# Dynamic convolution and squared-ReLU FFN on one core: second softmax part ahead of the first conv, its input loaded second, row moves on one queue a sub-block, blocks 0 to 4 reordered

## The chip, the cores and the metric

The kernel runs on one core of one Trainium2 chip. The metric is the time of one execution on the device, in microseconds (us). Each execution also reports the mean clock that the throttle granted to TensorE.

## The reference, cut to what matters

```python
# attention part: softmax of the given weights over K = 7 taps, then a causal dynamic convolution
w = softmax(weight_gen, axis=-1)                    # B=8, S=4096, H=8, K=7
out[b, s, h] = sum_k w[b, s, h, k] * x_pad[b, s + k, h]     # groups of 24 of the 192 channels
# FFN part, on 32768 tokens
h = maximum(x @ w_in, 0)                            # 192 -> 2048
return (h * h) @ w_out                              # 2048 -> 192
```

## The kernel before

The sequence is cut into 64 sub-blocks of 512 tokens. Blocks 0 and 1 hold one sub-block each, all later blocks two. For each sub-block, softmax weights (`exp` on ScalarE, called ACT; sum, reciprocal and products on VectorE, called DVE) are moved into rows by small DMAs (`wr`), DVE multiplies the rows by a band mask (`bd`), and TensorE (PE) convolves by matrix products with these bands (`C`, result `y`). A unit `u` is the first product for 256 columns of the FFN's hidden layer in blocks 0 and 1 and 128 in later ones (PE writes `h`, ACT applies ReLU to give `t`, DVE squares it to `g`). `M` is one half of a quarter's second product, collected in two PSUM banks `o`. The kernel spells out the order of these steps in strings.

The first sub-blocks get their softmax in small parts (`s0`, `s1`, `s2`: 8 rows for each of 128 partitions, with a halo of 6). The start of the program:

```python
spin(25)                        # idle products of 128x512, to keep TensorE busy
half_swap(); band_mask(); nc.gpsimd.memset(v_big, 0.0)
s0.load(nc.sync)                # 392 KB
load_w_in(w_st[0], 0, nc.sync)  # 768 KB in three DMAs
x_load_f32(0)                   # 480 KB
load_w_in(w_st[1], 1, nc.sync)  # 768 KB
s0.exp(0, s0.rh); s0.total(0, s0.rh); s0.recip(0, s0.rh); s0.scale(0, s0.rh, nc.vector)
nc.scalar.copy(out=w_i[:, 0, 0], in_=w_st[0])
wr_load_sbuf(0, [s0], (0, 2, 1, 4, 3), (nc.sync, nc.gpsimd))   # rows of sub-block 0: 5 DMAs of 16 KB
wr_load_sbuf(1, [s0], range(NT), (nc.gpsimd,))                 # rows of sub-block 1
x_cast(0, nc.scalar.copy)
cross_w_in_by_pe(0)
spin(14)
x_load_f32(1)
nc.scalar.copy(out=w_i[:, 1, 0], in_=w_st[1])
cross_w_in(1)
s1.load(nc.sync)                # the second softmax part's input, 392 KB, behind 16 other DMAs of SyncE
for i in (0, 2, 1, 3, 4):
    st_band(0, (i,))
st_conv(0)
# ... cut: loads of w_out, s2 and x ...
steady = "MuMuuu" * 3 + "MuuuMCu"
plans = {     # B bands, X cast of x, E exp, S rest of softmax, L load, C conv of the next block
    0: "B1 X1 u u u E1 S1 u C u u u u",
    1: "L3 u u B2 M E2 B3 u M E2 u u S2 u M u C u S2 M",
    2: "L4 u u u E3 M u u u M B4 u u u u M B5 S3 u u u u M u E3 C u",
    3: "L5 L6 M S3 u u u M u u u u M u M B6 E4 u u u M M B7 u u S4 u E4 M u C M u",
}
```

The M step that closes a quarter is followed by the copy that frees its banks:

```python
def o_sum(j, qt, ccs, o):
    # ... cut ...
    nc.scalar.copy(out=o_sb, in_=o[0][:, c])
    if len(o) == 2:
        nc.vector.tensor_tensor(out=o_sb, in0=o[1][:, c], in1=o_sb, op=AluOp.add)
```

The softmax here doesn't subtract the row's maximum and nothing guards it: scores larger than these inputs give would overflow.

## Time and profile before

| | before |
|---|---|
| time, median of 4 runs (three first, one more with the changed kernel) | 747.84 us (747.12 to 748.63) |
| span of the profiled run | 746.6 us, granted clock 1.000 |
| first useful matmul (conv 0) | 13.04 us |
| first unit | 15.55 us |
| start of the convs of blocks 2, 5, 6 | 33.13, 98.79, 121.34 us |

A row of a timeline is: start in us, length in us, engine, line of the kernel, operation, output and inputs, how many; in brackets, how long the engine was idle before it and what ended that. The prediction below shows the rows that carry it. ACT's timeline, for the arrival of w_in:

```profile
3.93 0.93 ACT L217 ACTIVATE ex<-wg 128x784 f32<-128x784 f32 x1 [1.83 <-DMA wg<-in_weight_gen_dram]
7.03 1.47 ACT L558 CAST w_i<-w_st 128x1536 f16<-128x1536 f32 x1 [2.17 <-DMA w_st<-in_moe_w_in_dram]
11.29 1.49 ACT L565 CAST w_i<-w_st 128x1536 f16<-128x1536 f32 x1
```

The first half of w_in is in at 7.0 us. The tile `wr` in the window from 8 to 12.2 us: the row moves by issuing engine, and how long they took from issue to landing (shortest, median, longest):

```profile
L330 POOL DMA_DIRECT2D wr<-v_first x7: 523/537/687, 8.6 to 11.8; - x7
L330 SPq DMA_DIRECT2D wr<-v_first x3: 597/598/636, 8.3 to 9.6; - x3
...
DMA to landing us min/median/max: 2.4/2.9/3.5
```

### The profile page before, as it was taken

Reading aid. Unit: us, or ns where it says so; the run is one execution under the profiler, and the core shown is the slowest. Engines: PE = TensorE matmul, PEld = TensorE weight load, DVE = VectorE, ACT = ScalarE, POOL = GpSimd, SP = SyncE. Lnnn points to the kernel's source line nnn. Section 1 sums busy time; section 2 is a strip of 40 time slices with the busy share of each in tenths; the row PEclk is TensorE's granted clock in tenths of the full one; section 3 lists DMA queues with packets and bytes.
Section 4 is the critical chain, followed back from the end, with each engine's and each line's share of the span. In section 5 each row is a group of like instructions: output and inputs, shape, how many; then the busy total and the mean of one; then the engine's idle time right before and its main releaser. Section 6 shows DMA issues by size and latency. Waiting matters only on the chain.

```text
span 746.6 us, 33289 instructions
## 1 busy us (share of the span) xinstructions
PE 739.0 (99%) x15106; PEld 556.5 (75%) x15106; DVE 621.8 (83%) x1001; ACT 624.7 (84%) x755; POOL 88.8 (12%) x130
## 2 busy tenths in 40 slices
PE   8999999999999999999999999999999999999998
PEld 4767877877777777777777777787777777777787
DVE  5999998998889888888889888898888987677853
ACT  5998788888888888888888888888888888888874
POOL 7321220101101100011000110001100011001000
PEclk9999999999999999999999999999999999999999
DMA  8654454436554234644245542365441354441312
GB/s 223 112 106 109 80 101 85 100 70 139 94 118 79 75 57 80 140 79 73 45 74 139 102 65 53 51 139 108 59 80 48 57 108 80 60 73 51 51 46 65
DMA packets 122169, 64.81 MB, mean 87 GB/s; under 512 B 83849, under 2 KB 118636, under 8 KB 121516
## 3 DMA queue, kind: packets, MB, share of 16 engines
q1 hardware_dynamic: 77708, 45.66, 22.4%
q0 software_dynamic: 44176, 16.93, 20.5%
q8 instruction: 118, 1.93, 1.1%
q14 instruction: 23, 0.19, 0.1%
q10 hardware_dynamic: 144, 0.10, 0.0%
HBM read 48.61 MB, written 28.70 MB: 104 GB/s over the span
## 4 chain that ended last, share of the span: by engine, by line
PE 94%; DVE 2%; issue 1%; DMA 1%; ACT 1%; POOL 0%; DVEq 0%; ACTq 0%
PE o L475 45%; PE h L441 43%; PE yp L416 6%; DVE g L453 1%; DVE bd L348 1%; DMA wr<-v_first 0%; DMA wg<-in_weight_gen_dram 0%; POOL wr L330 0%; ACT t L450 0%; DVE v_first L239 0%; ACT ex L217 0%; DVE ssum L224 0%; DVE rcp L231 0%; DVE o_sb L491 0%; ACT y L427 0%
## 5 line engine op out<-in xcount | busy, mean ns | idle before, releaser
L450 ACT ACTIVATE t<-h 128x1024 f16<-128x1024 f32 x512 | 496.7, 1026 | 65.6 <-PE h L441 65.3
L453 DVE TENSOR_TENSOR g<-t 128x1024 f16<-128x1024 f16 x512 | 334.3, 687 | 100.5 <-ACT t L450 97.8
L475 PEld LDWEIGHTS <-g 64*128 64x128 f16 (+1 forms) x8032 | 352.3, 94 | 55.0 <-issue 4.8
L475 PE MATMUL o<-w_o,g 64*128 64x192 f16 (+1 forms) x8032 | 385.3, 243 | 0.9 <-DVE o_sb L491 0.6
L441 PE MATMUL h<-y,w_i 64*128 64x512 f16 (+1 forms) x3168 | 379.7, 370 | 2.2 <-ACT t L450 0.9
L441 PEld LDWEIGHTS <-w_i 64*128 64x128 f16 x3168 | 162.6, 94 | 117.2 <-issue 5.2
L348 DVE TENSOR_TENSOR bd<-wr,mask 128x4160 f16<-128x4160 f16 (+3 forms) x89 | 149.3, 1701 | 4.0 <-DMA wr<-v_first 4.0
L300 POOL DMA_DIRECT2D xt<-in_x_dram x62 | 51.2, 830 | 446.7 <-PE yp L416 423.7
L489 ACT COPY o_sb<-o 128x384 f32<-128x384 f32 x129 | 62.2, 482 | 33.8 <-PE o L475 33.8
L491 DVE TENSOR_TENSOR o_sb<-o,o_sb 128x384 f32<-128x384 f32 x123 | 68.2, 555 | 8.4 <-ACT o_sb L489 5.6
L427 ACT CAST y<-yp 128x1024 f16<-128x1024 f32 (+1 forms) x64 | 48.1, 803 | 14.5 <-PE yp L416 14.5
L416 PE MATMUL yp<-bd,xt 128*32 128x104 f16 (+8 forms) x3864 | 51.7, 208 | 0.3 <-DVE bd L348 0.2
L416 PEld LDWEIGHTS <-xt 128*32 128x32 f16 (+3 forms) x3864 | 46.2, 92 | 6.7 <-issue 6.2
L239 DVE TENSOR_TENSOR v_big<-ex,rcp 128x112 f16<-128x112 f32 (+1 forms) x136 | 27.3, 263 | 1.8 <-DMA vd<-v_big 0.6
L217 ACT ACTIVATE ex<-wg 128x448 f32<-128x448 f32 (+2 forms) x44 | 27.2, 618 | 1.8 <-DMA wg<-in_weight_gen_dram 1.8
L224 DVE TENSOR_REDUCE ssum<-ex 128x64 f32<-128x448 f32 (+2 forms) x44 | 26.1, 594 | 2.5 <-ACT ex L217 2.3
L231 DVE RECIPROCAL rcp<-ssum 128x64 f32<-128x64 f32 (+2 forms) x44 | 23.7, 539 | 1.5
L290 POOL DMA_DIRECT2D xt<-in_x_dram x7 | 3.8, 549 | 135.8 <-PE yp L416 135.8
L330 POOL DMA_DIRECT2D wr<-v_first x31 | 16.8, 561 | 16.3 <-DVE v_first L239 16.1
L539 PE MATMUL wp<-warm 128*128 128x512 f16 x39 | 11.4, 459 | 1.3 <-DVE warm L531 1.3
L539 PEld LDWEIGHTS <-warm 128*128 128x128 f16 x39 | 4.3, 114 | 7.6 <-issue 3.5
L239 DVE TENSOR_TENSOR v_first<-ex,rcp 128x112 f16<-128x112 f32 (+1 forms) x48 | 9.1, 255 | 0.3
(24 smaller groups left out, 28.2 us busy)
## 6 DMA issues: line engine op xcount, KB each, us to landing
out_dram<-o_sb SPq DMA_DIRECT2D x63, 384.0 KB, 3.0
xt<-in_x_dram POOLq DMA_DIRECT2D x42, 240.0 KB, 5.9
wg<-in_weight_gen_dram SPq DMA_DIRECT2D x4, 1064.0 KB, 8.3
xt<-in_x_dram POOLq DMA_DIRECT2D x20, 192.0 KB, 5.6
wr<-vd SPq DMA_DIRECT2D x38, 80.0 KB, 3.6
vd<-v_big SPq DMA_DIRECT2D x5, 512.0 KB, 5.5
wg<-in_weight_gen_dram SPq DMA_DIRECT2D x5, 392.0 KB
wg<-in_weight_gen_dram SPq DMA_DIRECT2D x3, 616.0 KB, 4.1
```

Of the source, the lines that this page charges most:

```text
L217: nc.scalar.activation(out=self.ex[:, lo:hi].rearrange("p r g k e -> p (r g) k e"), in_=self.wg[:, lo:hi].rearrange("p r (g e) k -> p (r g ...
L239: eng.tensor_tensor(out=bass.AP(tensor=v.tensor, offset=v.offset + lo * H * SL + lo % SL * 2 + g * SL * 2, ap=[list(v.ap[0]), [H * SL + 2, ...
L300: eng.dma_start(out=dst[:, first:last], in_=ap)
L348: nc.vector.tensor_tensor(out=bd_t[j][:, H * lo : H * (lo + len(tiles) * n)].rearrange("p (g m c) -> p g m c", g=shape[1], c=2 * SL), in0= ...
L416: nc.tensor.matmul(out=yps[k // per][p0 : p0 + m, col + a : col + b], lhsT=x_t[s][:, i, 32 * q : 32 * q + m], rhs=bd[:, h // 2, h % 2, a - ...
L427: nc.scalar.copy(out=y[:, k0:k1, 0:th], in_=yp[:, 0 : (k1 - k0) * th].rearrange("p (k c) -> p k c", c=th),)
L441: nc.tensor.matmul(out=h[:, half, jj * th : (jj + 1) * th], lhsT=w_in_chunk(u * per + jj, slot, half), rhs=y_t[j][r0 : r0 + RT, k, 0:th], ...
L450: nc.scalar.activation(out=t1, in_=h, func=ActF.Relu)
L453: nc.vector.tensor_tensor(out=g, in0=t1, in1=t1, op=AluOp.mult)
L475: nc.tensor.matmul(out=oo[:, cc * Dm : (cc + 1) * Dm], lhsT=g[r0 : r0 + n, cc * P : (cc + 1) * P], rhs=w_o[r0 : r0 + n, fc, :], start=(fc ...
L489: nc.scalar.copy(out=o_sb, in_=o[0][:, c])
L491: nc.vector.tensor_tensor(out=o_sb, in0=o[1][:, c], in1=o_sb, op=AluOp.add)
```

## The change

Its intent: DVE waits 3.3 us at the start for rows. The second part's softmax is to fill this hole, which takes an exp and 3.3 us of DVE work out of block 0. For this its input is loaded second. The rows of sub-blocks 0 to 3 each go through one queue, GpSimd's and SyncE's in turn. Blocks 0 to 4 get other orders, with an M already in block 0. (The diff's first hunk only takes the tile of the exps from a pool with two buffers in place of one.)

```diff
--- before.py
+++ after.py
@@ -205,7 +205,7 @@
         def exp(self, lo, hi):
 
             if lo == 0:
-                self.ex = self.tile(p_one, p_one, "ex", HK, "ex8").rearrange(
+                self.ex = self.tile(p_one, p_sm, "ex", HK, "ex8").rearrange(
                     "p (r g k e) -> p r g k e", g=HP, k=KK, e=2
                 )
                 self.ssum, self.rcp = (
@@ -544,6 +544,7 @@
         band_mask()
         nc.gpsimd.memset(v_big, 0.0)
         s0.load(nc.sync)
+        s1.load(nc.sync)
         w_st = [
             p_wg.tile([P, (R + HALO) * HK], f32, name="w_st", tag="wg")[:, 0 : NQ + NQ // 2]
             for q in (0, 1)
@@ -551,21 +552,23 @@
         load_w_in(w_st[0], 0, nc.sync)
         x_load_f32(0)
         load_w_in(w_st[1], 1, nc.sync)
-        s0.exp(0, s0.rh)
-        s0.total(0, s0.rh)
-        s0.recip(0, s0.rh)
-        s0.scale(0, s0.rh, nc.vector)
+        for s in (s0, s1):
+            s.exp(0, s.rh)
+            s.total(0, s.rh)
+            s.recip(0, s.rh)
+            s.scale(0, s.rh, nc.vector)
         nc.scalar.copy(out=w_i[:, 0, 0], in_=w_st[0])
-        wr_load_sbuf(0, [s0], (0, 2, 1, 4, 3), (nc.sync, nc.gpsimd))
-        wr_load_sbuf(1, [s0], range(NT), (nc.gpsimd,))
+        wr_load_sbuf(0, [s0], range(NT), (nc.gpsimd,))
+        wr_load_sbuf(1, [s0], range(NT), (nc.sync,))
         x_cast(0, nc.scalar.copy)
         cross_w_in_by_pe(0)
         spin(14)
         x_load_f32(1)
         nc.scalar.copy(out=w_i[:, 1, 0], in_=w_st[1])
         cross_w_in(1)
-        s1.load(nc.sync)
-        for i in (0, 2, 1, 3, 4):
+        wr_load_sbuf(2, [s0, s1], range(NT), (nc.gpsimd,))
+        wr_load_sbuf(3, [s0, s1], range(NT), (nc.sync,))
+        for i in range(NT):
             st_band(0, (i,))
         st_conv(0)
 
@@ -578,12 +581,13 @@
 
 
 
+        orders = {4: "MuuuMuuuMMuuMuuMuuMuuuMCu"}
         steady = "MuMuuu" * 3 + "MuuuMCu"
         plans = {
-            0: "B1 X1 u u u E1 S1 u C u u u u",
-            1: "L3 u u B2 M E2 B3 u M E2 u u S2 u M u C u S2 M",
-            2: "L4 u u u E3 M u u u M B4 u u u u M B5 S3 u u u u M u E3 C u",
-            3: "L5 L6 M S3 u u u M u u u u M u M B6 E4 u u u M M B7 u u S4 u E4 M u C M u",
+            0: "B1 X1 u u u u C B2 u u u M u",
+            1: "L3 u u u B3 M u u u E2 S2 M u E2 S2 C u M",
+            2: "L4 u u u M E3 u B4 u u M u u u B5 u M u u u u M u C S3 M E3 u",
+            3: "L5 L6 u u u M S3 u u u M M u u M B6 M u B7 u u u M E4 u u M u S4 C u",
         }
 
 
@@ -596,9 +600,9 @@
         PIECE = 8
 
         TIMES = {
-            (1, 0): ((3, 15), (4, 0)),
+            (1, 0): ((3, 15), (4, 3)),
             (1, 1): ((4, 15), (5, 0)),
-            (1, 2): ((4, 1), (5, 1), (5, 15)),
+            (1, 2): ((4, 6), (5, 1), (5, 15)),
             (2, 0): ((6, 1), (6, 15), (7, 0)),
             (2, 1): ((7, 9), (7, 15), (8, 15)),
             (3, 0): ((9, 9), (9, 15), (10, 9), (10, 15), (11, 0)),
@@ -608,7 +612,7 @@
 
             if u == 0:
                 return j - 1, 12
-            return j, {1: 0, 7: 3, 9: 4, 15: 8}[u]
+            return j, {1: 0, 3: 1, 6: 4, 7: 3, 9: 4, 15: 8}[u]
 
         for n, s in enumerate(parts):
             piece = s.rh if n < 2 else PIECE
@@ -629,12 +633,12 @@
         for j in range(len(plans), NBLK - 1):
             a = BLOCKS[j + 1][0]
             small = [p for p in parts if p.fb <= j + 1][-1].r == FIRST
-            us = {6: (7, 9)}.get(j, (5, 9) if small else (1, 5))
+            us = {4: (10, 12), 6: (7, 9)}.get(j, (5, 9) if small else (1, 5))
             for n, u in enumerate(us):
                 at(j, u, "B", a + n)
         for j in range(len(plans), NBLK):
             plan, u = [], 0
-            for step in steady:
+            for step in orders.get(j, steady):
                 if step == "u":
                     plan += [f"{kind}{n}" for kind, n in fill.get((j, u), ())]
                     u += 1
```

## The prediction

> **What bounds the kernel now.** I read the page first: busy shares, then the chain that ended last.
>
> ```profile
> PE 739.0 (99%) x15106; PEld 556.5 (75%) x15106; DVE 621.8 (83%) x1001; ACT 624.7 (84%) x755; POOL 88.8 (12%) x130
> ...
> PE 94%; DVE 2%; issue 1%; DMA 1%; ACT 1%; POOL 0%; DVEq 0%; ACTq 0%
> ```
>
> TensorE (PE) is busy 99% of 746.6 us and is 94% of the chain. The granted clock is 9 tenths or more in all 40 slices. So the program is TensorE work plus a start, and the question is how much of the stretch that the change touches is not TensorE work at its own pace. The timeline of PE gives the pace. In the steady stretch (here blocks 5 and 6) each row starts when the one before it has been issued, so I take differences of starts, not the durations, whose ends are modelled:
>
> ```profile
> 102.95 1.48 PE L475 MATMUL o<-w_o,g 64*128 64x192 f16 x32
> 104.27 2.11 PE L441 MATMUL h<-y,w_i 64*128 64x512 f16 x18
> 106.21 1.48 PE L475 MATMUL o<-w_o,g 64*128 64x192 f16 x32
> ...
> 121.34 1.57 PE L416 MATMUL yp<-bd,xt 128*32 128x104 f16 x120
> 122.84 0.82 PE L441 MATMUL h<-y,w_i 64*128 64x512 f16 x6
> ```
>
> An M step (half a quarter of the second product) takes 104.27 - 102.95 = 1.32 us, three u steps (units of the first product) 1.94 us, so 0.65 each, and a conv C of two sub-blocks 1.50 us. A steady block, 16 u + 8 M + C = 10.35 + 10.56 + 1.50 = 22.4 us; convs of later blocks start 22.55 us apart (144.41, 166.96, 189.52). Nothing is left to win after block 6, and the diff doesn't touch it. The loss must sit in the start and in blocks 0 to 4. The PE timeline of the start and of block 0:
>
> ```profile
> 9.92 3.19 PE L539 MATMUL wp<-warm 128*128 128x512 f16 x14
> 13.04 0.51 PE L416 MATMUL yp<-bd,xt 128*32 128x104 f16 x26
> 13.72 0.94 PE L416 MATMUL yp<-bd,xt 128*32 128x104 f16 x46 [0.17 <-DVE bd L348]
> 15.55 2.80 PE L441 MATMUL h<-y,w_i 64*128 64x256 f16 x48 [0.89 <-ACT y L427]
> 18.41 0.91 PE L416 MATMUL yp<-bd,xt 128*32 128x104 f16 x72
> 19.32 0.83 PE L441 MATMUL h<-y,w_i 64*128 64x256 f16 x12
> 21.05 4.28 PE L441 MATMUL h<-y,w_i 64*128 64x256 f16 x60 [0.90 <-ACT t L450]
> 25.26 1.50 PE L475 MATMUL o<-w_o,g 128*128 128x192 f16 x16
> ```
>
> The reader is to see three things. Useful work starts at 13.04 (conv 0) and the units at 15.55. At 20.15 PE waits 0.90 us for ScalarE (ACT), all three PSUM buffers of h being full. Then 5 units (60 matmuls) take 25.26 - 21.05 = 4.21 us where 5 x 0.69 = 3.45 would do (0.69 from 28.88 to 30.95, 36 matmuls = 3 units): 0.76 us more, ACT's pace of 0.95 us a unit. After 25.26 PE has one more wait in the touched part, of 0.62 us in block 4 (below). Check by a sum, from the first unit (15.55) to the conv of block 6 (121.34), 105.8 us: 16 u x 0.69 + 63 u x 0.65 + conv 1 at 0.91 + 4 C x 1.50 + 8 M of the first two blocks at 1.43 + 24 M x 1.32 = 11.0 + 41.0 + 0.9 + 6.0 + 11.4 + 31.7 = 102.0. So the excess is 3.8 us: 0.90 + 0.76 + 0.62 = 2.3 are the waits named, 1.5 is small change at transitions, about 0.1 each. **2.3 us, 0.3% of the time, is all that the reordering can openly win.**
>
> **What the Trainium skill says.** "Perfetto Trace Analysis", Identifying the Most-Contended Engine: matmul busy share is no measure of the distance to the peak; gaps are to be sought stage by stage. The trace agrees: between 21.05 and 25.26 PE is shown busy while it runs at 3.45/4.21 of its pace. "DMA: Bandwidth & Descriptors", Issuing engines are not separate DMA queues: issuing from several engines saves only the sequencer's issue time, as all run on the same 16 DMA engines. In the trace a row move takes 0.55 us to issue on GpSimd and 0.60 on SyncE. The same page, Anatomy of one DMA: some 2.0 us fixed per DMA. Here a 16 KB row move lands 1.7 to 3.9 us after its issue, median 2.5, and about 3.0 at 8.3 us, when loads still fill the DMA engines (share 0.94 to 1.10 from 3 to 10 us).
>
> **The change part by part.**
>
> 1. Second softmax part moved ahead of conv 0. Removed from block 0: on ACT one exp of 128x784 (0.95 us), on VectorE (DVE) the sum 0.97, the reciprocal 0.85 and eight products 1.45 = 3.3 us. Put where? These rows of the DVE timeline tell:
>
> ```profile
> 6.79 1.46 DVE L239 TENSOR_TENSOR v_first<-ex,rcp 128x112 f16<-128x112 f32 x8
> 11.57 2.60 DVE L348 TENSOR_TENSOR bd<-wr,mask 128x832 f16<-128x832 f16 x5 [3.32 <-DMA wr<-v_first]
> 14.89 2.36 DVE L348 TENSOR_TENSOR bd<-wr,mask 128x3328 f16<-128x3328 f16 x2 [0.73 <-DMA wr<-v_first]
> ```
>
> DVE is idle 8.25 to 11.57, 3.32 us, for the rows to land; 3.3 us of softmax fits to within 0.1. On ACT there is a wait from 4.87 to 7.03 for w_in, and the exp (0.95) fits in it if its input has come. So nearly free at both ends.
>
> 2. The input of it loaded second: 392 KB more ahead of w_in and x on SyncE's queue. From 3.91 (first input) to 7.03 (first half of w_in, 768 KB) the queue moves 250 KB/us, so what follows comes 1.2 to 1.5 us later (estimate): the w_in cast on ACT starts at about 8.4 instead of 7.03, x's cast ends at 10.8 instead of 9.4, PE's swap products and the 14 spins end at about 13.9 instead of 13.1, the second w_in cast ends at about 13.8 instead of 12.78. All of these still end before the last band of conv 0 (next point), so they are hidden, with little to spare.
>
> 3. Row moves on one queue a sub-block. Before, conv 0's five moves were split, 3 on SyncE and 2 on GpSimd, issued within 1.9 us. Now all five are GpSimd's: 8.55 + 0.69 + 4 x 0.55 = 11.4 for the last issue's end, landing about 2.5 to 2.9 after its start (10.85): 13.5. Its band, 0.55 us, ends at about 14.2 (five bands from 11.6 in row would end at 14.17, as before). So conv 0 ends at about 14.8 against 14.66. Sub-block 1 gains: its moves go from SyncE at 8.3 rather than GpSimd at 9.8, so the 0.73 us wait at 14.89 goes. First unit at 15.55 + 0.2 (range 0 to +0.8): **+0.2**.
>
> 4. Block 0 in its new order, worked out from the first unit at 15.75 with ACT at 0.95 a unit and y at 0.82, PE at 0.69, three h buffers: ACT's four outputs end at 17.55, 18.5, 19.45, 20.4, y at 21.2. PE: four u to 18.55, conv 1 to 19.46, u to 20.16, u waits for 20.4, u waits for 21.2 and ends 21.9. Here the plan puts an M (1.43) where before there was none until ten units were done; ACT catches up meanwhile. Then u, and three u of block 1, to 26.1, M. 11 u + conv 1 + M = 7.6 + 0.9 + 1.4 = 9.9 us of work in 10.35: a loss of 0.45 in place of 1.66. **-1.2.** DVE takes the bands of sub-blocks 2 and 3 (2.3 us each) earlier, with the 3.3 us less; t1 has 5 buffers, so DVE may lag by several units before ACT stalls.
>
> 5. Blocks 3 and 4 in another order. The wait in block 4:
>
> ```profile
> 77.57 0.24 PE L475 MATMUL o<-w_o,g 64*128 64x192 f16 x1
> 78.43 1.48 PE L475 MATMUL o<-w_o,g 64*128 64x192 f16 x31 [0.62 <-DVE o_sb L491]
> ```
>
> An M that opens a quarter needs both o banks. They come free 1.53 us after the closing M ended (76.85 to DVE's add ending 78.38), and only one u (0.72) lay between. The new order puts u, C, u there (2.8 us): **-0.6**. But it has two u only (1.30 us) after a closing M in three places, one in block 3 and two in block 4: 1.53 - 1.30 = 0.23 each, more where DVE lags: **+0.6** for all three. M counts by the end of block 4 are 24 in both, u and C are the same.
>
> Sum: +0.2 - 1.2 - 0.6 + 0.6 = -1.0 us. From 748.4: **747.3 us**, with a trace span near 745.6.
>
> **The rivals.** (a) The start becomes the bound: if the 392 KB push w_in's second half or the GpSimd rows back by more than the slack of point 2, conv 0 and everything move by the same; DMA share is 1.00 there, which speaks for it. It would make 748 to 750. Against: rows from GpSimd landed in 2.9 us even then. (b) ACT stays the bound of block 0 whatever its order: 8 units, y and no exp are 8.4 us against PE's 6.4; then only the exp's 0.95 goes and the time is 747.5 to 748. Against: M gives ACT 1.43 us to catch up. (c) DVE lag: 9.86 of 10 us busy between 30 and 40 already; its work is only moved, so the M's that wait for o banks may lose all of the 1.8 us. Time 748.5. (d) All goes well and the transitions' 1.5 us shrink too: 745.3.
>
> **Range and chances.** The three runs of before spread over 1.5 us (747.12 to 748.63). With these rivals 8 in 10 lie in 745.0 to 749.4. 2% is 15 us, which is as long as the whole start: faster by over 2% is not to be had, since only 3.8 us are in excess there, and for slower a new stall of 15 us would be needed.
>
> **What would show it.** In the changed trace: DVE's wait before the first band down from 3.3 us to under 0.5, with the second part's products in it; first unit at 15.6 to 16.3; the w_in cast at about 8.4; an M at about 22 and at most 0.6 us lost in block 0; no wait at the first M of block 4, small waits (0.2 to 0.5) for o_sb at M's two units after a closing one; the conv of block 6 at about 120.3 in place of 121.34, and later convs 22.55 apart as before. The prediction is wrong if the conv of block 0 starts after 15, if the first M waits for w_o, whose four loads GpSimd issues only after the rows, or if a band comes late to a conv.

## The result and the profile after

The changed kernel took 750.57 us (median of 4 runs, 749.98 to 751.29) against 747.84. The ratio is 1.0037, with a 95% interval of 1.0019 to 1.0054. All ratios here are the mean time of one kernel's fast runs over the mean of the other's fast runs of the same rounds, so they are not quite the ratio of the medians quoted. The change is thus slower by nearly 3 us (0.4%). That is within 2%, as forecast, but outside the stated range of 745.0 to 749.4, and of the opposite sign to the predicted gain.

The page of the changed kernel, busy shares and chain:

```profile
PE 739.9 (99%) x15106; PEld 567.9 (76%) x15106; DVE 622.4 (83%) x1001; ACT 624.3 (83%) x755; POOL 89.4 (12%) x129
...
PE 95%; DVE 2%; ACT 1%; DMA 1%; issue 0%; SPq 0%; ACTq 0%; DVEq 0%
```

Little in these shares tells the two kernels apart. The PE timeline of the start does:

```profile
1.26 7.43 PE L539 MATMUL wp<-warm 128*128 128x512 f16 x25 [1.26 <-DVE warm L531]
11.01 0.81 PE L144 MATMUL pt<-w_i,swap 128*128 128x512 f16 x3 [2.31 <-ACT w_i L560]
11.65 4.87 PE L539 MATMUL wp<-warm 128*128 128x512 f16 x14
16.45 0.91 PE L416 MATMUL yp<-bd,xt 128*32 128x104 f16 x72
18.41 2.80 PE L441 MATMUL h<-y,w_i 64*128 64x256 f16 x48 [1.04 <-ACT y L427]
21.27 0.91 PE L416 MATMUL yp<-bd,xt 128*32 128x104 f16 x72
22.19 2.44 PE L441 MATMUL h<-y,w_i 64*128 64x256 f16 x36
24.56 1.49 PE L475 MATMUL o<-w_o,g 128*128 128x192 f16 x16
```

The first unit comes at 18.41 in place of 15.55. PE has a gap of 2.31 us for w_in, and the 14 spins after it take 4.87 us where they took 3.19. From 18.41 on, block 0 has no wait worth naming. DVE and ACT of the same stretch:

```profile
10.12 1.46 DVE L239 TENSOR_TENSOR v_first<-ex,rcp 128x112 f16<-128x112 f32 x8
13.90 4.87 DVE L348 TENSOR_TENSOR bd<-wr,mask 128x832 f16<-128x832 f16 x7 [2.32 <-DMA wr<-v_first]
```

```profile
9.49 1.47 ACT L560 CAST w_i<-w_st 128x1536 f16<-128x1536 f32 x1 [3.35 <-DMA w_st<-in_moe_w_in_dram]
13.68 1.47 ACT L567 CAST w_i<-w_st 128x1536 f16<-128x1536 f32 x1 [0.43 <-DMA w_st<-in_moe_w_in_dram]
```

The second part's products do fill DVE's hole (10.12 to 11.58), but the hole has grown: the first band starts at 13.90 in place of 11.57. And w_in comes at 9.5, not 7.0 as before nor 8.4 as predicted. The view of the tile `wr` in the same window, 8 to 12.2 us:

```profile
L330 POOL DMA_DIRECT2D wr<-v_first x7: 523/548/687, 8.6 to 12.0; - x7
L330 SPq DMA_DIRECT2D wr<-v_first x5: 597/599/637, 8.8 to 11.4; - x5
...
DMA to landing us min/median/max: 3.9/4.6/5.2
```

The rows are issued at the same moment as before, but land 4.6 us later at the median, not 2.9. The busy time by stretches of one us gives the clock (after the engines' columns: granted clock, mean busy share of the DMA engines, GB/s):

```profile
12.00:13.00 1.00, 1.00 (x4) 0.29 (x2) 0.00 (x0) 1.00 (x2) 1.00 (x2) 0.50 0.66 98
13.00:14.00 1.00, 1.00 (x4) 0.32 (x3) 0.10 (x1) 0.57 (x2) 0.09 (x1) 0.50 0.23 41
14.00:15.00 1.00, 1.00 (x4) 0.41 (x3) 1.00 (x3) 1.00 (x1) 0.91 (x2) 0.50 0.61 146
15.00:16.00 1.00, 1.00 (x6) 0.40 (x4) 1.00 (x3) 0.15 (x1) 0.67 (x2) 0.85 0.83 266
```

After the gap TensorE runs at half clock for some 3.4 us (three whole stretches and parts of the two around them). Last, the conv of block 5 in the PE timeline:

```profile
99.44 0.23 PE L416 MATMUL yp<-bd,xt 128*32 128x104 f16 x2
100.08 1.86 PE L416 MATMUL yp<-bd,xt 128*32 128x104 f16 x118 [0.41 <-DVE bd L348]
101.87 0.82 PE L441 MATMUL h<-y,w_i 64*128 64x512 f16 x6
```

It takes 101.87 - 99.44 = 2.43 us, where 1.50 to 1.53 is usual: its bands come late. DVE works on the last two of them until 100.49:

```profile
98.14 2.35 DVE L348 TENSOR_TENSOR bd<-wr,mask 128x3328 f16<-128x3328 f16 x2
```

Since both kernels have done the same number of units and M steps at the convs of blocks 2, 5 and 6, stretches between these starts can be compared directly. The four differences sum to the shift at the conv of block 6 (rounding aside):

| | before | changed | difference |
|---|---|---|---|
| first unit | 15.55 | 18.41 | +2.86 |
| first unit to conv of block 2 | 17.58 | 15.99 | -1.59 |
| conv of block 2 to conv of block 5 | 65.66 | 65.04 | -0.62 |
| conv of block 5 to conv of block 6 | 22.55 | 23.81 | +1.26 |
| conv of block 6 starts at | 121.34 | 123.25 | +1.91 |

The profiled spans differ by 2.9 us. The last 1.0 us of it is made of steps of 0.3 to 0.6 us late in the program, such as one at 194 us that the profile puts down to no wait but "issue". Such steps are in every trace at other places, so I don't count them as an effect.

### The profile page after: what moved, and what is told of

The parts are those of the page before. It is cut to its first block, busy times and chain, and to the rows that moved or that the text cites. A ratio compares the mean times of both kernels' runs of the same rounds, so it can differ in the third digit from the quotient of the medians.

```text
span 749.5 us, 33282 instructions
## 1 busy us (share of the span) xinstructions
PE 739.9 (99%) x15106; PEld 567.9 (76%) x15106; DVE 622.4 (83%) x1001; ACT 624.3 (83%) x755; POOL 89.4 (12%) x129
## 3 DMA queue, kind: packets, MB, share of 16 engines
q0 software_dynamic: 44144, 16.90, 20.1%
## 4 chain that ended last, share of the span: by engine, by line
PE 95%; DVE 2%; ACT 1%; DMA 1%; issue 0%; SPq 0%; ACTq 0%; DVEq 0%
PE o L475 45%; PE h L441 44%; PE yp L416 6%; DMA w_st<-in_moe_w_in_dram 1%; DVE bd L348 1%; DVE g L453 1%; ACT t L450 1%; PE wp L539 1%; DVE o_sb L491 0%; ACT w_i L560 0%; ACT y L427 0%; PE pt L144 0%; SPq L195 0%; SPq L129 0%; SPq L127 0%
## 5 line engine op out<-in xcount | busy, mean ns | idle before, releaser
L441 PEld LDWEIGHTS <-w_i 64*128 64x128 f16 x3168 | 172.4, 94 | 108.2 <-issue 3.8
```

The lines of the kernel that those rows point to most:

```text
L441: nc.tensor.matmul(out=h[:, half, jj * th : (jj + 1) * th], lhsT=w_in_chunk(u * per + jj, slot, half), rhs=y_t[j][r0 : r0 + RT, k, 0:th], ...
```

## The experiments

Theory S: the 392 KB in second place delay all that comes after them on the DMA engines, w_in and above all the small row moves, and the first band decides when conv 0 and the first unit come. Rival Q: the row moves on one queue are late of themselves. Rival C: the clock after PE's gap is the loss. Rival P: the new block orders lose the time. Theory B is for the conv of block 5: its bands were moved too late.

What the profiled execution of every kernel gave (us; C1 etc. are starts of the convs of blocks 1, 2, 5, 6; "clock" counts the timed runs with a mean granted clock of 0.998 or less):

| kernel | first band | first unit | difference | C1 to C2 | C2 to C5 | C5 to C6 | clock | ratio to before |
|---|---|---|---|---|---|---|---|---|
| before | 11.57 | 15.55 | 3.98 | 14.72 | 65.66 | 22.55 | 2 of 40 | 1 |
| changed | 13.90 | 18.41 | 4.51 | 13.13 | 65.04 | 23.81 | 4 of 4 | 1.0037 |
| e12 changed again | 14.06 | 18.04 | 3.98 | 13.12 | 65.08 | 23.82 | 2 of 5 | 1.0039 |
| e1 load second only | 13.93 | 17.91 | 3.98 | 14.73 | 65.69 | 22.52 | 1 of 6 | 1.0026 |
| e2 one queue only | 11.84 | 15.83 | 3.99 | 15.40 | 65.81 | 22.56 | 1 of 5 | 1.0014 |
| e3 short first spin | 11.37 | 15.35 | 3.98 | 14.73 | 66.32 | 22.54 | 5 of 6 | 1.0012 |
| e4 start only | 14.39 | 18.88 | 4.49 | 13.92 | 65.71 | 22.54 | 2 of 6 | 1.0025 |
| e5 bands earlier | 14.04 | 18.48 | 4.44 | 13.12 | 67.37 | 22.55 | 3 of 5 | 1.0031 |
| e6 longer first spin | 15.00 | 18.98 | 3.98 | 13.13 | 65.36 | 23.80 | 2 of 5 | 1.0043 |
| e7 load after w_in | 13.37 | 17.59 | 4.22 | 13.96 | 65.66 | 22.55 | 5 of 5 | 1.0039 |
| e8 blocks 2 to 4 only | 12.66 | 16.63 | 3.97 | 14.26 | 65.12 | 23.81 | 1 of 6 | 1.0012 |
| e9 load after rows | 11.27 | 15.93 | 4.66 | 14.17 | 67.00 | 22.55 | 0 of 5 | 1.0001 |
| e10 half second | 12.80 | 16.78 | 3.98 | 14.73 | 65.67 | 22.55 | 1 of 5 | 1.0031 |
| e11 tail swap | 12.09 | 16.07 | 3.98 | 14.73 | 65.08 | 22.56 | 0 of 5 | 0.9998 |

All gave correct results. Kernels with the start of before untouched (before, e8, e11) have their first band anywhere from 11.57 to 12.66, those with the whole changed start (changed, e4, e5, e6, e12) from 13.90 to 15.00: a start varies by about one us from execution to execution, and the two groups do not touch. Their means are 12.1 and 14.3, so the 2.33 us between the two first profiles are no accident, but shifts of the first band under one us can't be told from this spread. The stretches behind the start agree better, with one exception: e3 has 66.32 from C2 to C5 with the steps of the kernel before.

### e1: the load's place alone

```diff
         s0.load(nc.sync)
+        s1.load(nc.sync)
...
         cross_w_in(1)
-        s1.load(nc.sync)
```

> The kernel before with one thing changed: the input of the second softmax part is loaded second; its softmax stays in block 0. Theory S (the 392 KB ahead of w_in and x delay everything of the start): first half of w_in lands at about 9.4 us in place of 7.0, the rows of sub-block 0 land at 13 to 14 us in place of 11.5, first unit at about 18.4 in place of 15.6, granted clock 0.5 for about 3 us after 11, time +2.5 to +2.9 us on before. Rival Q (the row moves on one queue are what is late): nothing of this, time within 0.5 us of before. Rival P (the new order of blocks loses the time): within 0.5 us of before too.

Measured: 750.87 us against 748.82, ratio 1.0026 (1.0011 to 1.0040), some 2 us where 2.5 to 2.9 were expected. DVE and PE:

```profile
13.93 4.87 DVE L348 TENSOR_TENSOR bd<-wr,mask 128x832 f16<-128x832 f16 x7 [5.37 <-DMA wr<-v_first]
```

```profile
10.73 0.81 PE L144 MATMUL pt<-w_i,swap 128*128 128x512 f16 x3 [1.73 <-ACT w_i L559]
11.38 3.18 PE L539 MATMUL wp<-warm 128*128 128x512 f16 x14
```

This one move gives the whole delay of the rows: first band at 13.93, first unit 2.36 us later than before, kept up to the last conv (711.71 against 709.34). DVE's wait is now 5.37 us, as its hole has nothing in it. The lowered clock, which I had expected too, was absent in the profiled run (spins in 3.18 us) and in five of six runs. So the clock isn't needed for the loss. Rivals Q and P are out as its cause: neither the queues nor the orders were touched.

### e2: one queue a sub-block alone

```diff
-        wr_load_sbuf(0, [s0], (0, 2, 1, 4, 3), (nc.sync, nc.gpsimd))
-        wr_load_sbuf(1, [s0], range(NT), (nc.gpsimd,))
+        wr_load_sbuf(0, [s0], range(NT), (nc.gpsimd,))
+        wr_load_sbuf(1, [s0], range(NT), (nc.sync,))
```

> The kernel before with one thing changed: rows of sub-block 0 all from GpSimd in natural order, those of sub-block 1 all from SyncE. Theory S: rows land within 0.5 us of before (about 11.5 for the first, 13.5 for the last), first unit at 15.5 to 16.0, time within 0.5 us of before. Rival Q: first band at 13 us or later, time +2 us or more.

Measured: 749.96 us, ratio 1.0014 (1.0001 to 1.0027). First band +0.27, first unit +0.28, near the +0.2 of the prediction's point 3, but well within the spread of the starts, so the agreement proves little. Rival Q, which wanted the first band at 13 us or later, fell. The time was expected within 0.5 us of before and came out one us over. The other 0.7 us are in block 0, where PE's wait for ACT grew from 0.90 to 1.57 us: the second part's load was issued at 14.06 us (14.01 before), but landed at 20.1 only, and its exp held ACT for another 0.55 us. Why it took 6 us to land in this run is not shown. In the changed kernel this exp is no longer there.

### e3: a gap before w_in without any load moved

```diff
-        spin(25)
+        spin(14)
```

> The kernel before with 14 in place of 25 products in the first stretch of idle spinning, so that TensorE is idle for some 2.5 us before w_in comes, as in the changed kernel, while no load moves. Theory C (the idle gap alone lowers the granted clock and slows the 14 spins after it, which hold back conv 0): granted clock 0.5 for some 3 us after about 10 us, the second spins take 4.7 us in place of 3.2, conv 0 starts at about 14.8 in place of 13.0, time +1.0 us. Rival: the gap has no effect on the clock, second spins 3.1 us, time equal within 0.3 us.

Measured: 749.58 us, ratio 1.0012 (0.9996 to 1.0028): unclear. The profiled run had a gap of 3.13 us and kept full clock, so in it the expectation failed. But it was the exception: five of six runs show 0.997 or 0.998 and took 749.24 to 752.36 us, the one at 1.000 took 748.56. The kernel before shows such a clock in 2 of 40 runs, so the gap lowers the clock in most executions, not in all. Where in the program it fell in those five was not profiled. What it costs there, about one us by these times, is not shown.

### e4: the changed start with the old block orders

```diff
         # start as in the changed kernel; the plans of the kernel before, but
-            0: "B1 X1 u u u E1 S1 u C u u u u",
+            0: "B1 X1 u u u u C u u u u",
```

> The changed kernel's start (second part loaded and done ahead of conv 0, one queue a sub-block) with the block orders of the kernel before, its exp and softmax taken out of block 0. Theory S: first unit at about 18.4; the exp gone from block 0 gives back about 1 us; conv of block 2 at +1.7 to +2.0 us on before; time +1.2 to +2.0 us. Rival P (the block orders lose the time, the start is harmless): time at or under before.

Measured: 750.84 us, ratio 1.0025 (1.0012 to 1.0037). First band at 14.39, first unit at 18.88; the conv of block 2 came 2.5 us later than before, not 1.7 to 2.0. Taking exp and softmax out of block 0 gives back 0.80 us (C1 to C2: 13.92 in place of 14.72); the reordering of blocks 0 and 1 in the changed kernel gives another 0.79 (13.13). Both gains were real and smaller than the loss at the start. Rival P fell for the bulk of the loss.

### e5: the bands of block 5 earlier

```diff
-            us = {4: (10, 12), 6: (7, 9)}.get(j, (5, 9) if small else (1, 5))
+            us = {4: (8, 10), 6: (7, 9)}.get(j, (5, 9) if small else (1, 5))
```

> The changed kernel with the bands of sub-blocks 8 and 9 placed after units 8 and 10 of block 4 in place of 10 and 12. Theory B (these bands now come late to the conv of block 5, which waits for DVE and loses about 1 us): no wait of PE for bd before that conv, conv of block 6 0.8 to 1.2 us after-to-after nearer to conv of block 5 (22.6 us apart in place of 23.8), time 0.5 to 1.2 us under the changed kernel's (ratio to before about 1.0025). Rival: the loss at that conv is a single run's accident; distance of the convs 22.6 in the changed kernel's other runs too, time unchanged (ratio 1.0037).

Measured: 751.19 us, ratio 1.0031 (1.0019 to 1.0043), so no gain that could be told. The wait at the conv is gone (C5 to C6 is 22.55), but C2 to C5 is 2.3 us longer, 1.80 of it by one wait. PE:

```profile
95.12 0.24 PE L475 MATMUL o<-w_o,g 64*128 64x192 f16 x1
97.17 1.48 PE L475 MATMUL o<-w_o,g 64*128 64x192 f16 x31 [1.80 <-DVE o_sb L491]
```

The 2.4 us of band work now stand on DVE ahead of the add that frees the o banks. In the new order only two units (1.3 us) lie between a closing M and the next opening one, so the M waits 1.80 us. Theory B is right on where the wait came from, and wrong that an earlier place cures it: DVE's bands can delay either the conv or the M.

### e6: no gap before w_in

```diff
-        spin(25)
+        spin(35)
```

> The changed kernel with 35 in place of 25 products in the first stretch of idle spinning, so that TensorE has no gap before w_in comes. Theory S (rows land late; the clock is a minor part): granted clock 1.0 throughout, second spins 3.2 us in place of 4.8, but conv 0 still waits for its bands from 13.9 on, so the first unit comes at about 17.9 in place of 18.4, and the time falls by 0.5 us only. Rival C (the lowered clock is the main loss): first unit at 16 to 16.8, time down by 1.5 us or more.

Measured: 752.28 us, ratio 1.0043 (1.0031 to 1.0055). The profiled run had full clock and second spins of 3.18 us, as meant. Rows came at 15.00 in it, the latest of all, and the first unit 3.98 us after. The expected 0.5 us was not gained in time. Why the loads were slower in this execution is not known, and two of its runs still show 0.997. What it does tell: with full clock the first unit still waits for its bands (PE idle 0.72 us for `bd`), so rival C, as the main loss, is out.

### e7: the load behind w_in and x, ahead of the rows

```diff
         load_w_in(w_st[1], 1, nc.sync)
+        s1.load(nc.sync)
...
-        s1.load(nc.sync)
```

> The kernel before with the input of the second part loaded behind w_in and x but still ahead of the row moves. Theory S1 (small row moves land only when the bytes queued ahead of them on the DMA engines are through, whichever queue they come from): first w_in cast at 7.0 as before, but the rows land at 12.8 to 13.8 in place of 11.5, first unit at 16.8 to 17.9, time +1.2 to +2.2 us on before. Rival S2 (only what stands behind the load on SyncE's chain to conv 0, w_in and x, is late): first unit within 0.5 us of 15.6, time as before.

Measured: 751.80 us, ratio 1.0039 (1.0026 to 1.0052). w_in was cast at 7.70, nearly as early as before, yet the rows took a median of 4.1 us to land (3.8 to 4.9), and the first band came at 13.37:

```profile
7.70 1.47 ACT L559 CAST w_i<-w_st 128x1536 f16<-128x1536 f32 x1 [2.70 <-DMA w_st<-in_moe_w_in_dram]
```

```profile
13.37 4.87 DVE L348 TENSOR_TENSOR bd<-wr,mask 128x832 f16<-128x832 f16 x7 [4.98 <-DMA wr<-v_first]
```

That is later than any start without a load moved (11.37 to 12.66). So the rows are late with the load ahead of them even where w_in is not: S1 holds and S2 falls. Conv 0 now runs in pieces between bands, and the clock drops at about 15.5 us, shortly before the units begin. PE had been idle for only one us (13.05 to 14.01) and then busy for 65 to 71% of the time:

```profile
17.00:18.00 1.00, 0.41 (x6) 0.34 (x7) 1.00 (x2) 0.54 (x1) 1.00 (x3) 0.50 0.96 73
18.00:19.00 1.00, 1.00 (x12) 0.84 (x10) 0.98 (x2) 0.00 (x0) 1.00 (x2) 0.50 1.58 189
```

Four units take 5.0 us in place of 2.86. This would explain why it comes out slower than e1, though its rows are earlier (the intervals of the two overlap); all five runs show 0.995 to 0.997.

### e8: the orders of blocks 2 to 4 alone

```diff
+        orders = {4: "MuuuMuuuMMuuMuuMuuMuuuMCu"}
...        # plans 2 and 3, TIMES and band places of the changed kernel; start, plans 0 and 1 of before
```

> The kernel before with the changed orders of blocks 2 to 4 alone (and the times of the softmax pieces and bands that belong to them). Expected by the two traces: the 0.6 us wait for o banks in block 4 goes, about 1 us is lost at the conv of block 5, so the conv of block 6 comes 0.3 to 0.7 us later than before, time +0.2 to +0.8 us. Rival (these orders are a gain of 0.6 us or more): conv of block 6 at 120.8 or earlier.

Measured: 749.70 us, ratio 1.0012 (1.0000 to 1.0023). The wait of 0.6 us in block 4 is gone (C2 to C5 -0.54) and 1.26 us are lost at the conv of block 5, both as in the changed kernel, e6 and e12 (C5 to C6 within 0.02 in all four). Together +0.72 from C2 to C6: these orders lose on the whole. (The conv of block 6 itself started at 124.22, as this run's start fell late: first band at 12.66, with no line of the start changed, and a low clock in its first units. It is also the warning for reading single starts: w_in was cast at 8.37 in it, 1.3 us later than in the first profile of the same start.)

### e10: half of the load second

```diff
         s0.load(nc.sync)
+        s1.load_rows(0, 7, nc.sync)      # 7 of 14 rows: 196 KB
...
         cross_w_in(1)
-        s1.load(nc.sync)
+        s1.load_rows(7, s1.rh, nc.sync)
```

> The kernel before with half of the second part's input (196 KB) loaded second and the other half left in its old place; nothing else. Theory S (rows wait for the bytes ahead of them): first band about midway between 11.6 and 13.9, 12.4 to 13.2, first unit 3.98 later, time +0.7 to +1.6 us on before. Rival D (it is the additional transfer as such, or its place in SyncE's order, that costs): first band at 13.5 or later, time +2 us as with the whole load; or no effect at all, first band at 11.6.

Measured: first band at 12.80, just over half of the way from 11.57 to 13.93, first unit 3.98 us later, and every later stretch as in the kernel before. It looks as if the delay went with the bytes, but this trace can't show it: e8, with no load moved, has nearly the same start. The first bands of e8 and of this run:

```profile
12.66 4.87 DVE L348 TENSOR_TENSOR bd<-wr,mask 128x832 f16<-128x832 f16 x7 [4.36 <-DMA wr<-v_first]
```

```profile
12.80 4.87 DVE L362 TENSOR_TENSOR bd<-wr,mask 128x832 f16<-128x832 f16 x7 [4.40 <-DMA wr<-v_first]
```

The rows took a median of 3.5 us to land in both. The time was 750.79 us, ratio 1.0031 (1.0019 to 1.0044), 2.3 us more than before where the trace shows 1.2 and I had expected at most 1.6. That is no less than the whole load cost in e1 (1.0026). The profiled run was the fastest of the five, one other had a clock of 0.997. So rival D is not refuted: whether half of the bytes cost half of the time stays open.

### e9: the load behind the rows

```diff
         wr_load_sbuf(1, [s0], range(NT), (nc.gpsimd,))
+        s1.load(nc.sync)
...
         cross_w_in(1)
-        s1.load(nc.sync)
+        s1.exp(0, s1.rh)
...
-            0: "B1 X1 u u u E1 S1 u C u u u u",
+            0: "B1 X1 u u u S1 u C u u u u",
...        # in plan 3: "E4 M u C M u" becomes "E4 M M u C u"
```

> The kernel before with the second part's input loaded behind the row moves of sub-block 0 on SyncE's queue, its exp on ACT's idle time ahead of conv 0's y (12.8 to 14.7 us), its VectorE part left in block 0, and the two M steps of the last quarter in block 3 put side by side so that 2.8 us of other work lies ahead of the next quarter. Theory S (nothing queued ahead of the rows, so no delay): first band at 11.4 to 12.7 as in the kernel before, first unit 3.98 later, PE's 0.9 us wait in block 0 gone (conv of block 2 some 0.6 us nearer to the first unit than the 17.6 of before), the 0.6 us wait in block 4 gone; time 0.6 to 1.4 us under before. Rival: moving the exp gives nothing as ACT stays the bound, and the load at this place delays x or w_in of sub-block 1 instead; time as before or over.

Measured: 748.85 us against 748.17, ratio 1.0001 (0.9987 to 1.0014): a miss. The rows of sub-block 0 are on time (first band 11.27), and the waits in block 0 and block 4 that were to go are gone. But the load now stands ahead of the rows of sub-block 1 and of x. DVE:

```profile
16.17 2.36 DVE L348 TENSOR_TENSOR bd<-wr,mask 128x3328 f16<-128x3328 f16 x2 [2.30 <-DMA wr<-v_first]
```

It waits 2.30 us for the next rows where it waited 0.73, so x's cast ends later (conv 1 waits 0.64 us for it), the exp, fed at 14.26, pushes y back by 0.68, and conv 2 waits 1.42 us for its bands. The load has only handed its delay to the next in the queue.

### e11: two M steps side by side

```diff
-    3: "... u u S4 u E4 M u C M u",
+    3: "... u u S4 u E4 M M u C u",
```

> The kernel before with one thing changed: the two M steps of the last quarter in block 3 side by side ahead of the last unit and the conv, so that u, C, u lie between this quarter's end and the next one's start. Expected: PE's 0.6 us wait for o_sb at the start of block 4 gone, no new wait, first unit and conv of block 2 as before; time 0.3 to 0.9 us under before, which is below what five rounds can prove, so the trace is to decide. Rival: DVE's work piles up and the wait comes back elsewhere before the conv of block 6.

Measured: 748.76 us against 748.83, ratio 0.9998 (0.9986 to 1.0011). The trace shows the wait gone and no new one: C2 to C5 65.08 in place of 65.66, and C5 to C6 unchanged. A gain of 0.6 us is thus seen in this stretch of the trace and can't be proved by these times. This run's start fell 0.5 us late, so that its whole span, 746.7 us, is not under the 746.6 of the kernel before. Of all versions it alone gains in a stretch and loses in none that it touches.

### e12: the changed kernel once more

> The changed kernel itself, unaltered, once more, to see whether its start is the same in another execution. Theory S: first band at 13.9 to 15.0 and first unit 4.0 to 4.5 us later, granted clock 0.997 to 0.999 in most runs, the conv of block 5 waits for its bands again (conv of block 6 23.8 us after it), time +2.0 to +3.2 us on before. Rival: the lateness of the rows was an accident of one execution; first band at 12.5 or earlier.

Measured: 751.50 us against 748.83, ratio 1.0039 (1.0025 to 1.0052). First band 14.06, all stretches as in the first profile. This time the profiled run had full clock after a gap of 1.98 us, and the first unit came at 18.04, 3.98 us after the band. Against the first profile that is the clock's share: 4.51 - 3.98 = 0.5 us. e4 and e5, whose profiled runs had a low clock too, show the same (4.49 and 4.44).

## Why the prediction was wrong, point by point

**What bounds the kernel, and the pace.** Right. PE's pace outside the touched stretches is the same in all traces but for the odd late steps, and the start and blocks 0 to 5 hold the difference. The 2.3 us that it called the most to be won were nearly all won: 1.59 + 0.62.

**Point 1, the softmax in DVE's hole.** Right: it cost no DVE time ahead of the first band (it ended at 11.58, the band began at 13.90).

**Point 2 is the step that failed.** It said that what follows the load "comes 1.2 to 1.5 us later" and that all of it is "hidden, with little to spare". w_in came 2.46 us later (9.49 against 7.03; in the other traces 9.21 to 10.41 with the whole load second, 6.86 to 8.37 with no load moved). SyncE's issue of it was 0.45 us later (1.72 against 1.27). The sum divided 392 KB by a speed of 250 KB/us (which makes 1.6) as if each load had the DMA engines to itself in turn. Up to 7.0 us the kernel before had moved some 1.58 MB (the GB/s of its one-us stretches added up), where the two loads that had landed make 1.19 MB. So bytes of loads issued later move beside it. In the changed kernel it was some 2.2 MB up to 9.49, where the three landed loads make 1.59. That this sharing makes up the rest of the 2.46 us is argued from these sums; no run isolates it.

**Point 3, the rows,** took over that error: it had GpSimd's rows landing 2.5 to 2.9 us after issue, from the trace of before. The rows of the view above took 3.9 to 5.2. Their landing isn't a constant of a small move but depends on the load put ahead of them: e1 shows it with nothing else changed, e7 with w_in on time. Point 3's own matter, one queue, did no visible harm (+0.28 in e2 for +0.2, both below the spread of starts). The start's term was +0.2 and measured +2.86: 2.33 for the rows and 0.5 for the clock, which the prediction had not thought of. Conv 0 began at 16.45, and the prediction had named a start after 15 as a sign that it is wrong.

**Point 4, block 0.** Right in mechanism and a little small: -1.2 predicted, -1.59 measured, about half of it from the exp's removal and half from the order (e4).

**Point 5.** The wait for o banks went, -0.62 for -0.6. The three small waits of 0.2 us for o banks did not show as such. That the total there was too small has another cause: the conv of block 5 waited for bands, which the prediction named among what would make it wrong but did not size. The bands had been put after units 10 and 12, and DVE was still at them. This is 0.9 of the +1.26; another 0.2 is in the M behind that conv (102.53 to 104.08 in place of 1.32 us).

**The rivals.** (a), the start as the bound, is what happened. It was given 748 to 750, which 750.57 still exceeds, and too little weight. (b) is out: block 0 lost next to nothing. (c), DVE's lag, is the cause at the conv of block 5. The sum as predicted, 0.2 - 1.2 - 0.6 + 0.6 = -1.0 (from 748.4 that is 747.4, not the 747.3 of the text); as measured, 2.86 - 1.59 - 0.62 + 1.26 = +1.91 at the conv of block 6. The timed runs say +2.7; the 0.8 between are within what executions differ in, and are not assigned.

**The Trainium skill in it.** The prediction cited that all issuing engines share the same 16 DMA engines, and then used a landing time as if it were the move's own; the runs agree with the page (in e1 rows from both queues are late, 3.7 to 5.2 us, behind loads from SyncE alone). For the clock, "TensorE: Matmul & The Clock Gate", What's actually happening, describes a clock gate that halves the clock after an idle window of some 3.4 us on a free-running timer. The traces agree with half clock (0.50 for some 3.4 us), not with the length of the gap (2.31 us). The outcome changes from run to run (e3, and the changed kernel at 4 of 4 and 2 of 5 runs), as a free-running timer would have it, but no run shows the timer.

## What to carry to other kernels

Before loading something earlier, list what will queue behind it, small moves above all, and don't take their landing as a fixed latency; five moves of 16 KB held up the whole start. Take the spread of a stretch from traces in which it is unchanged before reading a small shift in it. A hole of 3 us on one engine that waits for DMA is not free when filling it needs more DMA. When a band or an add is moved on an in-order engine, check both consumers: here an earlier band delayed an M by 1.80 us, a later one the conv by about one.

## What the Trainium skill lacked or had wrong

- "DMA: Bandwidth & Descriptors", Anatomy of one DMA, gives a fixed part of some 2.0 us for one DMA; here moves of at most 16 KB between SBUF tiles, issued behind large loads, took 2.4 to 3.5 us in the kernel before and 3.9 to 5.2 in the changed one. The page gives no time for a small DMA behind large ones.
- The same page, SWDGE vs HWDGE vs iDMA, says that each DMA engine goes round robin between the internal queues that GpSimd's and SyncE's DMAs feed. One could hope from it that GpSimd's rows pass SyncE's backlog. In the changed kernel they landed no sooner than after 13 us, when w_in's second half had come (its cast began at 13.68).
- "TensorE: Matmul & The Clock Gate", What's actually happening, ties the fall of the clock to an idle window of some 3.4 us. Here it fell after a PE gap of 2.31 us, while a gap of 3.13 us in e3's profiled run left it at 1.00.
